# Attention with mixed heads and two dense stages on one core: where the splits of q and k, the conversion of w3 and the fold stand in the order of work

## The chip, the cores and the metric

The kernel runs on one core of one Trainium2 chip. The metric is the device time of one launch in microseconds, as the median of several runs. Beside it one execution was taken by the hardware profiler; its rows are what the argument rests on.

## What is computed

Four batches of attention (12 heads, 448 positions, 64 per head) whose scores are mixed across heads before and after the softmax, then two dense stages on the 1792 rows that come out. Shortened:

```python
scores = scale * np.matmul(q, k.transpose(0, 1, 3, 2))
scores = np.einsum('bhij,hg->bgij', scores, w_pre)
scores = scores - np.max(scores, axis=-1, keepdims=True)
attn = np.exp(scores)
attn = attn / (np.sum(attn, axis=-1, keepdims=True) + 1e-09)
attn = np.einsum('bhij,hg->bgij', attn, w_post)
x = np.matmul(attn, v)          # then laid out as 1792 x 768
a = x @ w1                      # 768 x 1024
b = x @ w2
h = a * b @ w3                  # 1024 x 1024
x2 = h @ w_out                  # 1024 x 768
h2 = x2 @ w_in                  # 768 x 2048
out = np.maximum(0.01 * h2, h2) @ w_out2
```

All weights of the dense stages arrive as float64, read as pairs of 32-bit words, and are converted to float32 on the chip.

## The kernel before

**Splits.** A matmul in full precision is made of three with rounded operands: a copy (hi) of the operand in a rounded type, written by ScalarE (`hi_act`, L76), and the rest (lo), subtracted on VectorE (`lo_dve`, L79). `split` (L82) issues both, one behind the other. The profile puts them at L77 and L80.

**Attention** (L118). Its instructions keep the order in which they are written (`manual_schedule`); each engine works through its own in that order. A batch has four chunks of query rows, three of 120 and one of 88 rows; a chunk has blocks of 10 rows, 12 blocks or 9, 180 in all. Blocks are written (b, c, t): batch, chunk, block of the chunk. For a block, `premix` (L227) mixes scores across heads by a matmul into `pm`, takes the maximum `mx` on VectorE and the exponential `e` with its sum on ScalarE; `sums` and `weigh` (L245, L249) turn the sum into weights `kr` by way of GpSimd (POOL); three blocks later (LAG) `postmix` (L260) mixes back into `po` and copies it to `ap`, on ScalarE for odd steps that are plain, otherwise on VectorE. `pm` and `po` have two PSUM banks each.

Scores come from `qk` (L184), two chunks ahead: a step computes two pairs of heads into `pq`, four copies to a tile `s` follow, and SP stores `s` to `sdr` in HBM; there are three tiles `s`. `relayout` (L211) loads them back as `sr`, for two blocks at a time, eight blocks ahead. Scores are computed at t in QT = (0, 6, 9), or (0, 5, 7) in the chunk with 9 blocks. The product with v, `av` (L279, tile `px`), of the chunk before comes in two halves at t = 3 and 4 (AT).

Around these stand the steps that feed them: `q_load` at t = 0 and `q_split` at t = 8 for the chunk three ahead; `k_load` of the next batch at t = 1, 2, 3 of chunk 1, `k_split` at its t = 7 to 11 and at t = 1 of chunk 2; `v_prep` (v's load) at t = 5 of chunk 0, and for the first batch ahead of the first scores of chunk 1. `conversions` (L303) turns w_out and w3 into float32 in HBM (`wof`, `w3f`) in 32 units of one copy `wc` on ScalarE (L96) and four operations on VectorE (L98 to L107): two steps of it at every t in QT or AT from block 14 on.

**Dense stages** (L416). Here a scheduler orders the instructions on each engine by its own estimate. `fold` (L436) multiplies w3 with w_out into `w34`, so that h is multiplied once: it loads the eight parts of `wof` (copies on ScalarE, subtractions on POOL, L442), and takes w3 in eight pieces, 48 matmuls `pw` each. In the same time `make_x` (L522) loads and splits the attention's result as x. Raw weights, `wof` and pieces of `w3f` share three buffers (tag `wr`). The scheduler was free to put the fold's loads and copies between the attention's last blocks.

Of the kernel before, what the change touches and what calls it, by code (L numbers as in the profile page):

```python
# [23 lines left out]
def attention_moe_kernel(ctx: ExitStack, tc, qt, kt, vt, w_pre, w_post, w1, w2, w3t, w_out, w_in2, w_out2, out):  # L24
# [39 lines left out]
    w3f = dram.tile([DF, DF], F32, name="w3f")  # L64
# [52 lines left out]

    def attention():  # L118
        with ExitStack() as es:
# [56 lines left out]
            def q_split(b, c):  # L176
                m = cols[c]
                qs = kv.tile([P, NPAIR, 2, CH], F32R, tag="qs", name="qs", bufs=2)
                t = qls.pop((b, c))
                hi_act(qs[:, :, 0, :m], t[:, :, :m])  # L180
                lo_dve(qs[:, :, 1, :m], t[:, :, :m], qs[:, :, 0, :m])
                qst[b, c] = qs

            def qk(b, c, p):  # L184
# [3 lines left out]
                if r == 0:  # L188
                    st[b, c] = big.tile([CH, 2 * HP, S], F32, tag="s", name="s", bufs=3)
# [21 lines left out]
            def relayout(n):  # L211
# [4 lines left out]
                if t % 2 == 0:  # L216
# [4 lines left out]
                    else:  # L221
                        nc.sync.dma_start(out=pair[:nb * H, 0], in_=sdr[b, c][o:o + nb].rearrange("i h j -> (i h) j"))
# [26 lines left out]
            def weigh(n):  # L249
# [5 lines left out]
                nc.gpsimd.tensor_scalar(  # L255
# [88 lines left out]
            filler = conversions()  # L344

# [6 lines left out]
            q_split(0, 0)  # L352
            k_split(0, 0)
            for p in range(NPAIR):
                if p + 1 < NPAIR:
                    k_split(0, p + 1)
                qk(0, 0, p)
                flush()
            q_split(0, 1)
            constants()  # L360
            for n in range(AHEAD):
                relayout(n)
            v_prep(0)
# [3 lines left out]
            q_split(0, 2)  # L367
            for n in range(NB + LAG):
                flush()
                plain = True  # L370
                if n < NB:
                    b, c, t, _ = blocks[n]
                    ci = order.index((b, c))
                    QT = (0, 6, 9) if len(chunks[c][2]) > 9 else (0, 5, 7)
# [12 lines left out]
                if m >= 0:  # L387
# [3 lines left out]
                    postmix(m, nc.scalar.copy if plain and n % 2 else nc.vector.tensor_copy)  # L391
                if n < NB:
                    if t == 0 and ci + QAHEAD + 1 < len(order):
                        q_load(*order[ci + QAHEAD + 1])
                    if t == 8 and ci + QAHEAD + 1 < len(order):
                        q_split(*order[ci + QAHEAD + 1])
                    if c == 0 and t == 5 and b > 0:
                        v_prep(b)
                    if b + 1 < B:
                        if c == NC - 3 and 1 <= t < 4:  # L400
                            k_load(b + 1, t - 1)
                        if c == NC - 3 and t >= 7:
                            k_split(b + 1, t - 7)
                        if c == NC - 2 and t == 1:
                            k_split(b + 1, 5)
                    if n >= START and not plain:
                        for _ in range(2):
# [8 lines left out]
    def moe():  # L416
        with ExitStack() as es:
# [117 lines left out]
            fold(unit)  # L535
# [108 lines left out]
```

## Time and profile before

| | us |
|---|---|
| median of 3 runs (lowest, highest) | 1443.58 (1442.26, 1443.80) |
| the profiled execution's own time | 1446.14 |
| its span, first to last instruction | 1444.2 |
| TensorE matmuls busy | 1371.5 (95%) |
| VectorE busy | 873.4 (60%) |
| ScalarE busy | 604.4 (42%) |
| GpSimd busy | 167.9 (12%) |

TensorE is the busy engine, and it is so over the whole span only on average: from about 550 us on it has no pause, ahead of that it has some in nearly every stretch. The granted clock of TensorE has a mean of 0.982 of full speed over the span, so there are stretches at half speed. The DMA engines are busiest in the attention. Engines off TensorE's path are idle much of the time; what counts of them is whether TensorE waits for what they make.

### The profile page before, as it was taken

How to read it: one execution, taken by the hardware profiler on the slowest of the kernel's cores; microseconds unless marked ns; L12 is line 12 of the kernel's file. 1: busy time of each engine (PE TensorE's matmuls, PEld its weight loads, DVE VectorE, ACT ScalarE, POOL GpSimd, SP SyncE). 2: the span in 40 equal slices, each digit the busy share in tenths (PEclk: the TensorE clock that was granted, in tenths of full speed). 3: DMA queues.
4: the chain of work that ended last, by engine and by line, in shares of the span. 5: the costliest groups of instructions: out<-in, count | busy, mean ns of one | idle time of the engine just before them, and what ended most of it. 6: DMA issues, size and time to landing. Idle time of an engine off the chain costs nothing.

```text
span 1444.2 us, 22126 instructions
## 1 busy us (share of the span) xinstructions
PE 1371.5 (95%) x8520; PEld 1184.1 (82%) x8520; DVE 873.4 (60%) x1530; ACT 604.4 (42%) x1167; POOL 167.9 (12%) x374
## 2 busy tenths in 40 slices
PE   5879997998999899999999999999999999999998
PEld 3646675766666579999999999999999999999998
DVE  4445665666666453466434967869566247686862
ACT  3545454664555443333322543525233224452330
POOL 0313232332323550000000000000000000000000
PEclk9899999999999899999999999999999999999999
DMA  8877996899798736633222434325442133432401
GB/s 238 260 202 189 278 286 192 239 294 271 199 297 260 200 103 189 200 100 107 59 86 97 129 112 132 91 95 169 151 129 88 44 109 104 137 113 85 153 1 77
DMA packets 140117, 226.23 MB, mean 157 GB/s; under 512 B 19245, under 2 KB 117549, under 8 KB 139565
## 3 DMA queue, kind: packets, MB, share of 16 engines
q1 hardware_dynamic: 140012, 224.83, 51.4%
q8 instruction: 67, 1.10, 0.3%
q14 instruction: 38, 0.30, 0.1%
HBM read 164.77 MB, written 60.03 MB: 156 GB/s over the span
## 4 chain that ended last, share of the span: by engine, by line
PE 80%; ACT 6%; DMA 5%; DVE 5%; issue 2%; SPq 1%; POOL 0%; ACTq 0%; DVEq 0%; POOLq 0%
PE pm L512 41%; PE po L579 16%; PE po L270 6%; PE px L290 5%; PE pw L450 5%; PE pm L233 4%; PE pq L194 3%; ACT e L240 2%; DMA sdr<-s 2%; DVE mx L237 2%; ACT s L201 1%; DMA sr<-sdr 1%; DMA wof<-wof 1%; DMA wr<-in_moe_w_out_dram 1%; ACT ap L277 1%
## 5 line engine op out<-in xcount | busy, mean ns | idle before, releaser
L512 PE MATMUL pm<-x,ws 128*128 128x448 f32 x2304 | 477.7, 368 | 0.0
L512 PEld LDWEIGHTS pm<-x,ws 128*128 128x128 f32 x2304 | 432.4, 188 | 43.3
L579 PE MATMUL po<-ws,g 128*128 128x384 f32 x1344 | 234.3, 334 | 0.0
L579 PEld LDWEIGHTS po<-ws,g 128*128 128x128 f32 x1344 | 233.2, 188 | 0.3
L270 PEld LDWEIGHTS po<-kr,e 120*112 120x112 f32 (+1 forms) x1440 | 172.6, 181 | 65.5 <-issue 50.8
L233 PE MATMUL pm<-sr,kpre 120*120 120x448 f32 x360 | 173.3, 564 | 44.3 <-ACT e L240 40.8
L240 ACT ACTIVATE e<-pm,mx 120x448 f32<-120x448 f32 x180 | 114.4, 636 | 216.2 <-DVE rc L253 197.6
L270 PE MATMUL po<-kr,e 120*112 120x120 f32 (+1 forms) x1440 | 187.8, 275 | 2.0 <-POOL kr L255 1.5
L255 POOL TENSOR_SCALAR kr<-kpost,rc 120x120 f32<-120x120 f32 x180 | 109.9, 610 | 299.4 <-DVE rc L253 261.9
L96 ACT ACTIVATE wc<-wr 128x768 f32<-128x768 f32 (+2 forms) x128 | 106.6, 836 | 85.8 <-DVE ws L80 57.9
L80 DVE TENSOR_TENSOR ws<-wc,ws 128x768 fp32r<-128x768 f32 x96 | 91.4, 954 | 82.6 <-ACT ws L77 81.4
L77 ACT ACTIVATE ws<-wc 128x768 fp32r<-128x768 f32 x96 | 80.7, 843 | 119.1 <-PE po L579 74.0
L237 DVE TENSOR_REDUCE mx<-pm 120x1 f32<-120x448 f32 x180 | 111.1, 618 | 25.2 <-PE pm L233 23.4
L277 DVE COPY ap<-po 112x480 f32<-112x480 f32 (+1 forms) x130 | 84.2, 648 | 61.1 <-PE po L270 60.1
L512 PE MATMUL pm<-h,ws 128*128 128x448 f32 x576 | 119.4, 368 | 0.0
L512 PEld LDWEIGHTS pm<-h,ws 128*128 128x128 f32 x576 | 108.1, 188 | 10.9
L107 DVE SCALAR_TENSOR_TENSOR wc<-wr,wc 128x768 uint32<-128x768 uint32 (+2 forms) x128 | 111.5, 871 | 2.0
L104 DVE SCALAR_TENSOR_TENSOR wc<-wr,wc 128x768 uint32<-128x768 uint32 (+2 forms) x128 | 110.9, 868 | 1.4
L290 PEld LDWEIGHTS px<-ap,vs 112*64 112x64 f32 x1536 | 78.0, 142 | 30.4 <-issue 15.2
L98 DVE TENSOR_SCALAR wc<-wc 128x768 f32<-128x768 f32 (+2 forms) x128 | 65.6, 513 | 53.7 <-ACT wc L96 53.7
L233 PEld LDWEIGHTS pm<-sr,kpre 120*120 120x120 f32 x360 | 53.2, 188 | 51.9 <-ACT e L240 47.0
L194 PEld LDWEIGHTS pq<-ks,qs 64*120 64x120 f32 (+1 forms) x576 | 51.3, 189 | 52.2 <-issue 24.3
(46 smaller groups left out, 1080.4 us busy)
## 6 DMA issues: line engine op xcount, KB each, us to landing
sr<-sdr SPq DMA_DIRECT2D x88, 420.0 KB, 8.1
sdr<-s SPq DMA_DIRECT2D x36, 840.0 KB, 6.6
wr<-in_moe_w_dram SPq DMA_DIRECT2D x32, 768.0 KB, 4.6
wr<-in_moe_w_in_dram SPq DMA_DIRECT2D x32, 768.0 KB, 4.6
wr<-in_moe_w_out_dram SPq DMA_DIRECT2D x32, 768.0 KB
wr<-in_moe_w_dram SPq DMA_DIRECT2D x16, 512.0 KB, 8.2
sdr<-s SPq DMA_DIRECT2D x12, 616.0 KB
wr<-in_moe_w_out_dram SPq DMA_DIRECT2D x16, 384.0 KB, 7.5
```

The source lines that it names most:

```text
L96: nc.scalar.activation(out=cf, in_=hi.bitcast(F32), func=ACTF.Abs)
L104: lambda: nc.vector.scalar_tensor_tensor(out=c, in0=hi, scalar=0xC0000000, in1=c, op0=ALU.bitwise_and, op1=ALU.bitwise_or),
L107: lambda: nc.vector.scalar_tensor_tensor(out=c, in0=lo, scalar=29, in1=c, op0=ALU.logical_shift_right, op1=ALU.bitwise_or),
L233: nc.tensor.matmul(pm[:r], kpre[:r, :nb, :].rearrange("p i h -> p (i h)"), sr[:r], start=True, stop=True)
L237: nc.vector.tensor_reduce(out=mx[:r], in_=pm[:r], axis=AX.X, op=ALU.max, negate=True)
L240: nc.scalar.activation(out=e[:r], in_=pm[:r], func=ACTF.Exp, bias=mx[:r], scale=1.0, accum_out=sm[:r])
L255: nc.gpsimd.tensor_scalar(out=kr[:r], in0=kpost[:r], scalar1=rc[:r], scalar2=None, op0=ALU.mult)
L270: nc.tensor.matmul(po[:, jc, :, :nb], e[:r, jc * JP:(jc + 1) * JP], kr[:r, :, :nb], start=True, stop=True,)
L277: copy(ap[:, :, :, o:o + nb], po[:, :, :, :nb])
L290: nc.tensor.matmul(px[e * D:(e + 1) * D, p - p0, :ni], vst[b][:, jc, 2 * p + e, :], ap[:, jc, 2 * p + e, :ni], start=(jc == 0), stop=(jc = ...
L512: nc.tensor.matmul(dst, wt[:, a, kk, :], x[:, kk, c, n * S:(n + 1) * S], start=(kk == 0 and j == 0), stop=(kk == kn - 1 and j == 2),)
L579: nc.tensor.matmul(po, g[:, m, a, t * P:(t + 1) * P], wts[m][:, c, 0, cs], start=(m == 0 and j == 0), stop=(m == FQ - 1 and j == 2),)
```

## The change

- `k_split` and `q_split` issue only the copy on ScalarE and return the subtraction, which the loop issues behind the step's postmix (`lows`). q's split stands at t = 3 (t = 8 in the first chunk), k's at t = 4 of chunk 1 (two) and t = 3 and 4 of chunk 2 (two each).
- `q_load` stands at t = 8, one chunk earlier; `k_load` at t = 0, 1, 6; `v_prep` at t = 4 of chunk 0, in the first batch too; only four relayouts stand ahead of the scores of chunk 1. In the first chunk QT is (5, 8, 10). `s` has four tiles.
- `conversions` has only the 16 units of w_out. A step in AT issues one step of it, one in QT two.
- ScalarE copies `ap` at t = 1, 5, 8, 10 where the step is plain.
- The fold loads w3 raw, 1 MB a piece, and converts it like the other weights. Its instructions on POOL and SP stand behind the attention's last `kr` and its last relayout of a single block.

```diff
 def k_split(b, p):
     kst[b, p] = kv.tile([P, 2, S], F32R, tag="ks", name="ks", bufs=NPAIR + 2)
-    split(kst[b, p], kls[b, p // 2][:, p % 2, :])
+    src, dst = kls[b, p // 2][:, p % 2, :], kst[b, p]
+    hi_act(dst[:, 0], src)
+    return lambda: lo_dve(dst[:, 1], src, dst[:, 0])
...
-    st[b, c] = big.tile([CH, 2 * HP, S], F32, tag="s", name="s", bufs=3)
+    st[b, c] = big.tile([CH, 2 * HP, S], F32, tag="s", name="s", bufs=4)
...
 units = [(w_out, wof, r, c0, DM // 2) for r in range(DF // P) for c0 in (0, DM // 2)]
-units += [(w3t, w3f, r, c0, DF // 2) for r in range(DF // P) for c0 in (0, DF // 2)]
...
-for n in range(AHEAD):
+for n in range(4):
     relayout(n)
-v_prep(0)
 for p in range(NPAIR):
     qk(0, 1, p)
     flush()
+for n in range(4, AHEAD):
+    relayout(n)
...
+if t == (LAG if ci else 8) and ci + QAHEAD + 1 < len(order):
+    lows.append(q_split(*order[ci + QAHEAD + 1]))
+if b + 1 < B and t in AT:
+    if c == NC - 3 and t == LAG + 1:
+        lows += [k_split(b + 1, p) for p in (0, 1)]
+    if c == NC - 2:
+        lows += [k_split(b + 1, p) for p in ((2, 3) if t == LAG else (4, 5))]
...
-postmix(m, nc.scalar.copy if plain and n % 2 else nc.vector.tensor_copy)
+postmix(m, nc.scalar.copy if plain and n < NB and t in (1, 5, 8, 10) else nc.vector.tensor_copy)
+while lows:
+    lows.pop(0)()
...
-w = {"w1": w1, "w2": w2, "wi": w_in2}[kind]
-return load_raw(wp, col_block(w, m), (KM, P), 3)
+w = {"w1": w1, "w2": w2, "wi": w_in2, "w3t": w3t}[kind]
+return load_raw(wp, col_block(w, m), (KF if kind == "w3t" else KM, P), 3)
...
-fold(unit)
+with tc.issue_after(ends["pool"].ins), tc.issue_after(ends["sync"].ins):
+    fold(unit)
```

First place, ScalarE in chunk (1, 1). Before, from t = 8 on (a number behind a name is that of the tile):

```order
L240 ACTIVATE e_2342,sm_2343<-pm_2338,mx_2340 120x448
L277 COPY ap_2188<-po_2352 112x48x10
L77 ACTIVATE qs_2358<-ql_2099 128x6x120
L77 ACTIVATE ks_2361<-kl_2125 128x448
L240 ACTIVATE e_2368,sm_2369<-pm_2364,mx_2366 120x448
L201 ACTIVATE s_2376<-pq_2377 88x448
L201 ACTIVATE s_2376<-pq_2378 88x448
L201 ACTIVATE s_2376<-pq_2387 88x448
L201 ACTIVATE s_2376<-pq_2388 88x448
L77 ACTIVATE ks_2403<-kl_2147 128x448
L240 ACTIVATE e_2416,sm_2417<-pm_2412,mx_2414 120x448
```

After, the same engine at t = 3 and 4 of chunk (1, 2):

```order
L243 ACTIVATE e_2514,sm_2515<-pm_2510,mx_2512 120x448
L76 ACTIVATE qs_2522<-ql_2341 128x6x120
L76 ACTIVATE ks_2524<-kl_2108 128x448
L76 ACTIVATE ks_2526<-kl_2108 128x448
L95 ACTIVATE wc_2566<-wr_2299 128x384
L243 ACTIVATE e_2572,sm_2573<-pm_2568,mx_2570 120x448
L76 ACTIVATE ks_2582<-kl_2295 128x448
L76 ACTIVATE ks_2584<-kl_2295 128x448
L243 ACTIVATE e_2626,sm_2627<-pm_2622,mx_2624 120x448
```

The copies of k, which stood one to a step between an exponential and the next, now stand two together, with q's, in the steps with the product with v.

Second place, SP after the first chunk's scores are stored. Before:

```order
L220 DMA sr_229<-sdr_0_0_57 120x2x448
L220 DMA sr_231<-sdr_0_0_57 120x2x448
L220 DMA sr_233<-sdr_0_0_57 120x2x448
L220 DMA sr_235<-sdr_0_0_57 120x2x448
L170 DMA vs_237<-in_v_dram 112x3072
L209 DMA sdr_0_1_58<-s_239 120x1792
L209 DMA sdr_0_1_58<-s_261 120x1792
L209 DMA sdr_0_1_58<-s_283 120x1792
L220 DMA sr_316<-sdr_0_0_57 120x2x448
```

After:

```order
L223 DMA sr_228<-sdr_0_0_57 120x2x448
L223 DMA sr_230<-sdr_0_0_57 120x2x448
L212 DMA sdr_0_1_58<-s_232 120x1792
L212 DMA sdr_0_1_58<-s_254 120x1792
L212 DMA sdr_0_1_58<-s_276 120x1792
L223 DMA sr_298<-sdr_0_0_57 120x2x448
L223 DMA sr_300<-sdr_0_0_57 120x2x448
L223 DMA sr_313<-sdr_0_0_57 120x2x448
L177 DMA ql_315<-in_q_dram 128x720
L223 DMA sr_341<-sdr_0_0_57 120x2x448
L223 DMA sr_374<-sdr_0_1_58 120x2x448
L173 DMA vs_382<-in_v_dram 112x3072
```

Two relayouts and v's load, which stood ahead of the stores of chunk 1, now stand behind them.

Third place, ScalarE at the seam between attention and fold. Before:

```order
L240 ACTIVATE e_5833,sm_5834<-pm_5829,mx_5831 120x448
L277 COPY ap_5759<-po_5841 112x48x10
L240 ACTIVATE e_5851,sm_5852<-pm_5847,mx_5849 120x448
L240 ACTIVATE e_5869,sm_5870<-pm_5865,mx_5867 96x448
L277 COPY ap_5759<-po_5877 112x48x10
L77 ACTIVATE ws_6028<-wf_6022 128x1024
L77 ACTIVATE ws_6033<-wf_6024 128x1024
L77 ACTIVATE ws_6094<-wf_6026 128x1024
L277 COPY ap_5759<-po_5893 112x48x10
L77 ACTIVATE x_6127<-xm_6128 128x448
L77 ACTIVATE x_6127<-xm_6160 128x448
```

After:

```order
L76 ACTIVATE wo_5844<-wof_5865 128x768
L76 ACTIVATE wo_5844<-wof_5869 128x768
L76 ACTIVATE x_6000<-xm_6001 128x448
L76 ACTIVATE x_6000<-xm_6033 128x448
L76 ACTIVATE wo_5844<-wof_5873 128x768
L95 ACTIVATE wc_5883<-wr_5877 128x1024
L95 ACTIVATE wc_5894<-wr_5879 128x1024
L76 ACTIVATE x_6000<-xm_6076 128x448
L76 ACTIVATE x_6000<-xm_6108 128x448
L76 ACTIVATE ws_5889<-wc_5883 128x1024
```

Before, eight copies of `wof` stand further up, among the exponentials, and the first copies of w3's pieces (`ws`) follow the last exponential. After, three stand further up and five behind the last exponential (three of them here), then two conversions of w3's pieces (`wc`) and copies of x, and then the first copy `ws`. On POOL the eight subtractions of `wof` stood among the last blocks and now stand in a row behind the last `kr`.

## Rows read from the trace of the kernel before

**Rows 1.** Chain of waits, merged: start us, us, what (with number of pieces).

```profile
44.98 1.49 PE pm L233 x2
...
52.94 0.82 PE po L270 x8
...
54.52 0.82 PE po L270 x8
...
59.27 0.82 PE po L270 x8
...
148.05 1.00 PE po L270 x8
...
152.42 1.00 PE po L270 x8
...
172.49 2.04 PE px L290 x48
...
201.57 2.68 PE px L290 x48
...
239.95 3.92 PE px L290 x48
...
299.83 2.04 PE px L290 x48
...
456.19 2.68 PE px L290 x48
...
522.88 2.68 PE px L290 x48
...
549.96 62.27 PE pw L450 x358
```

**Rows 2.** Timeline of PE, 62 to 116 us: first product of chunk (0,1).

```profile
68.80 2.68 PE L290 MATMUL px<-ap,vs 112*64 112x120 f32 x48
```

**Rows 3.** Waits of PE, 0 to 550 us: total us, times, longest.

```profile
PE pm L233 <- ACT e L240: 40.8, 26, 10.7
```

**Rows 4.** Windows: busy us of each engine, then PEclk, DMA share, GB/s.

```profile
40.00:45.00 5.00, 3.47 (x11) 2.61 (x12) 0.86 (x3) 2.81 (x8) 1.67 (x5) 0.50 0.95 332
...
400.00:450.00 50.00, 47.08 (x430) 34.09 (x427) 33.79 (x75) 26.65 (x66) 15.60 (x36) 1.00 0.97 293
```

**Rows 5.** The tile kl: k copies, k subtractions, their waits, landing of k loads.

```profile
L77 ACT ACTIVATE ks<-kl x24: 560/576/622, 5.3 to 364.9; 128x448 fp32r<-128x448 f32 x24
...
L80 DVE TENSOR_TENSOR ks<-kl,ks x24: 617/624/626, 5.9 to 365.5; 128x448 fp32r<-128x448 f32 x24
...
  ACT ks L77: 25.0, 18
...
DMA to landing us min/median/max: 4.1/8.4/12.7
```

**Rows 6.** Groups by shape, 0 to 560 us: count | busy us, mean ns | idle before.

```profile
L442 POOL TENSOR_TENSOR wo<-wof,wo 128x768 fp32r<-128x768 f32 x8 | 14.4, 1805 | 8.4 <-DMA wof<-wof 6.7 <-ACT wo L77 1.5
...
L96 ACT ACTIVATE wc<-wr 128x512 f32<-128x512 f32 x16 | 11.1, 691 | 0.0
...
L104 DVE SCALAR_TENSOR_TENSOR wc<-wr,wc 128x512 uint32<-128x512 uint32 x16 | 10.9, 681 | 0.0
```

**Rows 7.** Timelines of SP and ACT: start us, us, [idle before <- releaser].

```profile
23.55 1.28 SPq L209 DMA_DIRECT2D sdr<-s  x3
...
39.02 1.85 ACT L201 ACTIVATE s<-pq 120x448 f32<-120x448 f32 x4 [11.39 <-DMA sdr<-s]
...
81.66 0.54 ACT L96 ACTIVATE wc<-wr 128x384 f32<-128x384 f32 x1 [11.46 <-DMA wr<-in_moe_w_out_dram]
```

**Rows 8.** Timeline of POOL: two kr, beside VectorE's L104 and last.

```profile
480.57 1.59 POOL L255 TENSOR_SCALAR kr<-kpost,rc 120x120 f32<-120x120 f32 x1 [0.40 <-PE po L270]
...
538.56 0.58 POOL L255 TENSOR_SCALAR kr<-kpost,rc 96x120 f32<-96x120 f32 x1 [0.36 <-DVE rc L253]
```

**Rows 9.** Page, DMA issues: count, KB each, median us to landing.

```profile
wr<-in_moe_w_dram SPq DMA_DIRECT2D x32, 768.0 KB, 4.6
```

More of the change, by code (lines that the diff above doesn't have):

```diff
@@ L116, in convert @@
         return cf
+    ends = {}
     def attention():
@@ L179, in q_split @@
                 t = qls.pop((b, c))
+                qst[b, c] = qs
                 hi_act(qs[:, :, 0, :m], t[:, :, :m])
-                lo_dve(qs[:, :, 1, :m], t[:, :, :m], qs[:, :, 0, :m])
-                qst[b, c] = qs
+                return lambda: lo_dve(qs[:, :, 1, :m], t[:, :, :m], qs[:, :, 0, :m])
             def qk(b, c, p):
@@ L221, in relayout @@
                     else:
-                        nc.sync.dma_start(out=pair[:nb * H, 0], in_=sdr[b, c][o:o + nb].rearrange("i h j -> (i h) j"))
+                        ends["sync"] = nc.sync.dma_start(out=pair[:nb * H, 0], in_=sdr[b, c][o:o + nb].rearrange("i h j -> (i h) j"))
                     srt[n] = pair[:, 0, :]
@@ L254, in weigh @@
                 kr = wk.tile([IB * H, H, IB], F32, tag="kr", name="kr", bufs=4)
-                nc.gpsimd.tensor_scalar(
+                ends["pool"] = nc.gpsimd.tensor_scalar(
                     out=kr[:r], in0=kpost[:r], scalar1=rc[:r], scalar2=None, op0=ALU.mult
@@ L344, in attention @@
             filler = conversions()
+            lows = []
             q_load(0, 0)
@@ L351, in attention @@
             q_load(0, 2)
-            q_split(0, 0)
-            k_split(0, 0)
+            q_split(0, 0)()
+            k_split(0, 0)()
             for p in range(NPAIR):
                 if p + 1 < NPAIR:
-                    k_split(0, p + 1)
+                    k_split(0, p + 1)()
                 qk(0, 0, p)
                 flush()
-            q_split(0, 1)
+            q_split(0, 1)()
             constants()
-            for n in range(AHEAD):
+            for n in range(4):
                 relayout(n)
-            v_prep(0)
             for p in range(NPAIR):
@@ L366, in attention @@
                 flush()
-            q_split(0, 2)
+            for n in range(4, AHEAD):
+                relayout(n)
+            q_split(0, 2)()
             for n in range(NB + LAG):
@@ L373, in attention @@
                     ci = order.index((b, c))
-                    QT = (0, 6, 9) if len(chunks[c][2]) > 9 else (0, 5, 7)
+                    QT = (5, 8, 10) if ci == 0 else (0, 6, 9) if len(chunks[c][2]) > 9 else (0, 5, 7)
                     plain = t not in QT and t not in AT
@@ L390, in attention @@
                         av(*blocks[m - tt - 1][:2], tt)
-                    postmix(m, nc.scalar.copy if plain and n % 2 else nc.vector.tensor_copy)
+                    postmix(m, nc.scalar.copy if plain and n < NB and t in (1, 5, 8, 10) else nc.vector.tensor_copy)
+                while lows:
+                    lows.pop(0)()
                 if n < NB:
[L393 to L397, printed above, removed]
-                        v_prep(b)
[L399 to L405, printed above, removed]
+                    if c == 0 and t == 4:
+                        v_prep(b)
+                    if (t == 8 or n == 0) and ci + QAHEAD + (1 if n == 0 else 2) < len(order):
+                        q_load(*order[ci + QAHEAD + (1 if n == 0 else 2)])
+                    if b + 1 < B and c == NC - 3 and t in (0, 1, 6):
+                        k_load(b + 1, (0, 1, 6).index(t))
                     if n >= START and not plain:
-                        for _ in range(2):
+                        next(filler, None)
+                        if t in QT:
                             next(filler, None)
@@ L463, in load_w @@
             def load_w(kind, m):
-                if kind in ("w34", "w3t"):
+                if kind == "w34":
                     t = wp.tile([P, KF, P], F32, tag="wr", name="wf", bufs=3)
-                    src = w3f if kind == "w3t" else w34
-                    nc.sync.dma_start(out=t, in_=src[:, m * P:(m + 1) * P].rearrange("(k p) m -> p k m", p=P))
+                    nc.sync.dma_start(out=t, in_=w34[:, m * P:(m + 1) * P].rearrange("(k p) m -> p k m", p=P))
                     return t
```

5 lines of the change are left out of this document (2 added, 3 removed).

## Prediction

> **What bounds the kernel now.** I read the chain of waits first. From 549.96 us on it is TensorE alone: the rest of the fold's 384 matmuls (358 in 62.27 us) and then the dense stages without a break [rows 1]. The change adds no matmul there, so all it can win lies in the attention ahead of it, and all it can lose there too or at the seam.
>
> In the attention I price a chunk as if TensorE never waited. A plain step is 54.52 - 52.94 = 1.58 us. Two steps of which one computes scores take 59.27 - 54.52 = 4.75, so scores add 1.59. A step with the product with v takes 152.42 - 148.05 = 4.37, so it adds 2.79 [rows 1]. A chunk of 12 blocks with three groups of scores and two products is 12 x 1.58 + 3 x 1.59 + 2 x 2.79 = 29.3 us, one of 9 blocks 24.6, one of 12 without scores 24.5. The reader should now look at the first product with v of each chunk, which stands at t = 3 and so marks the chunks. 172.49 to 201.57 is 29.1: as priced. 201.57 to 239.95, the chunk that carries five of the six k splits, is 38.4. Summed over marks [rows 1, 2]: 68.80 to 172.49 takes 103.7 against 83.2 (20.5 lost), 172.49 to 299.83 takes 127.3 against 112.5 (14.8), 299.83 to 456.19 takes 156.4 against 141.8 (14.6), 456.19 to 522.88 takes 66.7 against 53.8 (12.9). That is **62.8 us** above the price of TensorE's own work. TensorE's waits for the exponentials e are 40.8 us of it in 26 waits [rows 3]; the rest is smaller waits and the clock, which is granted at 0.50 (1.2 GHz) after a long wait [rows 4]. Attention is therefore bound by TensorE in quiet chunks and by the in-order queues of ScalarE and VectorE in busy ones.
>
> **The change, part by part.** *Splits.* Now a k split puts its subtraction on VectorE right behind its copy on ScalarE: VectorE waited 25.0 us in 18 places for these copies, and in its queue the next block's maximum stands behind the subtraction, and e behind that [rows 5]. The step becomes a loop through two engines. Afterwards q's and k's copies stand in the two steps with the product with v, and the subtractions behind that step's copies out of PSUM. Does it fit? The fullest such step has one q and two k splits. ScalarE: two k copies at 0.576, a q copy (720 columns for 448, so 0.93) and one conversion of at most 0.69 [rows 5, 6], 2.8 us. VectorE: two at 0.624, q 1.0, one conversion step of at most 0.68, 2.9 us. The product with v gives 2.79 us of TensorE's time [rows 1]: just covered, and a chunk has only two such steps. If the cover is gone, each microsecond over it is a microsecond of TensorE. The bounds are nothing left of the loss and all of it; I take 0.25 us left in each of 12 chunks (3 us), since the chunk at 172.49, which has conversions and a q split and no k split, already runs as priced. The q split is also earlier: the first scores of a batch no longer wait for a split issued one step before.
>
> *Start.* ScalarE waits 11.39 us until 39.02 for a store out of the score tiles, because four relayouts and v's load were queued on SP ahead of the stores issued at 23.55, and three buffers were taken [rows 7]. With four buffers, two relayouts and no v ahead of the stores, and chunk 2's scores moved from t = 0 to t = 5, blocks 0 to 3 no longer wait for it. Block 4 now waits instead: its relayout (0.43 MB, 120 x 896 floats) is queued behind two others and three stores of 0.86 MB (120 x 1792). 3.9 MB from about 22 us at 250 to 293 GB/s (the latter what a full window moves [rows 4]) land at 35 to 38 us. Block 4's premix then starts near 37.5 where it stood at 44.98 [rows 1], 7.5 earlier, but has one group of scores more behind it (1.59): a gain of 6 (3 to 9).
>
> *Conversions.* Half of the units (w3: 8.4 MB read, 4.2 MB written) leave the attention, and one unit's step is issued in the steps with v where there were two. ScalarE's 11.46 us wait at 81.66 for the first raw weight [rows 7] shrinks, since the load now has a whole step with v before it is used, but doesn't vanish: I leave 4 us (0 to 8) of that chunk's loss. What moves into the fold is costed there.
>
> *k loads.* They move from t = 1, 2, 3 to t = 0, 1, 6, and the first two splits from t = 7, 8 to t = 4. Landing took 4.1 to 12.7 us, median 8.4 [rows 5]; from the end of t = 0 to t = 4 there are about 2 x 1.58 + 4.37 + 1 = 8.5. A late one stops ScalarE by up to 4 us, three times; TensorE is two blocks ahead. Costed at nothing, 12 at most.
>
> *The fold queues behind the attention.* Before, its loads and copies stand among the last blocks, and ScalarE waits there for wof: the 12.9 us above. After, three loads are issued behind the last relayout, and two copies still stand eight exponentials before the end. With scores and their stores done a load of this size should land in little more than the 4.1 us that a k load took at least [rows 5]. TensorE can go on for two blocks (3.2 us), so 4 us (1 to 8) of the 12.9 stay.
>
> Now the price. The eight subtractions on POOL, 1.805 us each [rows 6], all start behind the last kr. Let T be its end, 538.56 + 0.58 = 539.1 before [rows 8]. Before, TensorE's fold block starts in effect at 549.96 less 26 matmuls of 62.27/358 = 0.174, 545.4, or T + 6.3. After: three buffers serve wof and the raw w3, so the first piece of w3 is loaded when the sixth subtraction is done (six of 1.805, and half a microsecond of waiting, T + 11.3) and the second at T + 13.6. A piece is 1 MB; 768 KB take 4.6 us [rows 9]. Both pieces, 2.1 MB, are there at T + 19 (293 GB/s) to T + 24 (768 KB in 4.6 us); I take T + 21. On ScalarE the copy of piece one stands behind the conversion of piece two and two copies of x (the third place in the change's section): 1.4 + 1.2 + 1.4 us at most, by twice the 512-column row and the 448-column row. TensorE starts at T + 25 (T + 21 to T + 31). That is 18.7 us later against T than before. It then runs at the low clock for a while: the window from 40 to 45, in which a long wait ends, is wholly at 0.50 [rows 4]; 3 us. **21.7 us lost** (17 to 30).
>
> Later pieces are covered: 48 matmuls take 8.35 us, a piece costs VectorE five operations of at most 1.36 us (twice 0.681 [rows 6]), 6.8 us.
>
> A rule weighed: POOL's kr takes 1.59 us beside VectorE's L104 and 0.58 alone [rows 6, 8]. The Trainium skill, "SBUF — State Buffer", section "Who interferes with whom", says that a GpSimd operation and a VectorE operation with two SBUF inputs exclude each other for a whole instruction; the trace agrees, with these 1.59 us. By it the two subtractions for x that VectorE does beside POOL's eight would delay the fold by up to 2 x 0.62 = 1.2 us, and the sum would be 1408 instead of 1407.
>
> **Sum.** Attention: 62.8 - 3 - 4 - 4 + 6 = 57.8 us won. Seam: 21.7 lost. Net 36.1. The profiled execution took 1446.1 (span 1444.2 and 1.9 around it), 2.5 above the median of 1443.6; the same work is gone from either, so I take it off the median: **1407**, 1410 for a profiled execution.
>
> **Rivals.** *The stalls move (0.17).* The steps with v are filled to 2.9 of 2.79 us, and k loads may land late. If half of the three losses of 14.6 to 20.5 stays (about 17 us with the late loads), 1407 + 17 = 1424. For it: the cover is that thin. Against: the next steps are plain and have slack on both engines.
>
> *A better seam and start (0.14).* If SP's queue is idle at the end, the w3 pieces land at T + 17 and the fold starts at T + 20, and the two waits that I left (4 and 4) go too: 1407 - 13 = 1394.
>
> *The fold is fed too slowly (0.05), slower than before.* ScalarE and SP work in order, and in the fold a piece's copy stands among copies of x and of results. Traffic is 8.4 MB of w3, 2.8 of x and 3.1 of results in 67 us, 213 GB/s, against 167 GB/s for one load alone (768 KB in 4.6 us). If pieces come every 13 us instead of 8.35, and TensorE idles at each, eight cost 37 us, the whole gain: the point from which it decides. At 13.5 the time is 1407 + 41 = 1448.
>
> *The attention is set by DMA (0.04).* A full window has a DMA share of 0.97 [rows 4]. If transfers set the chunks, the moved splits win nothing before the conversions end, and only the 12.6 MB taken out count, 12.6/0.293 = 43 us less: the start's 6 and the tail's 9 would be in it, so 1444 - 43 + 22 = 1423. Against: the chunks that run as priced have the same share.
>
> **How the numbers follow.** Forecast, 1397 to 1418: 0.60. The seam's bounds (17 to 30) and the start's (3 to 9) make most of its width. Rivals 0.17, 0.14, 0.05, 0.04. The range 1388 to 1428 takes in all but the slow fold and the tails of the others, about 0.15. About 0.2% (3 us) is what a measurement of this kernel can tell from no change. Faster 0.94, within it 0.01, slower 0.05.
>
> **What would show it.** Right: marks 29 to 30 us apart in chunks with 12 blocks, no wait over 2 us on e between 100 and 460, SP's stores of chunk 1 ahead of v, one gap of 15 to 25 us on TensorE before the fold's first matmul, then 66 to 70 us of fold and dense stages as long as before. Wrong: waits on e in the steps after t = 3 and 4, ScalarE waiting for kl, gaps on TensorE inside the fold.

## The result

| | before | after |
|---|---|---|
| median (lowest, highest), us | 1443.69 (1442.26, 1446.25) | 1403.22 (1398.96, 1403.41) |
| ratio, 95% interval | | 0.9711 [0.9688, 0.9734] |
| profiled execution, us | 1446.14 | 1403.05 |
| its span, us | 1444.2 | 1401.3 |

The change is faster by 40.5 us in the medians and by 42.9 in the spans of the profiled executions. The prediction was 1407, with 1388 to 1428 around it.

### The profile after

In the changed kernel the maximum `mx` is L240, `e` L243, `kr` L258, the products with v L293, the splits L76 (copy) and L79 (subtraction), the conversion L95 to L106, `wof`'s subtractions on POOL L449 and the fold's matmuls L457. The page gives TensorE as busy for 97% of the span where it was 95%. Its row of granted clocks (40 slices of 35 us, in tenths of full speed) is below 9 in the first slice, the start, and in the two around 490 us, the seam, and nowhere between.

```profile
PEclk8999999999999879999999999999999999999999
```

The chain of waits (start, us, what) gives the marks of the prediction, the first product with v of a chunk, to be set beside [rows 1]:

```profile
37.23 1.82 PE pm L236 x2
...
64.18 2.68 PE px L293 x48
...
148.42 2.01 PE px L293 x48
...
261.51 2.01 PE px L293 x48
...
401.51 2.68 PE px L293 x48
...
429.27 2.68 PE px L293 x48
...
456.22 2.68 PE px L293 x48
...
500.80 68.54 PE pw L457 x380
```

64.18 to 148.42 takes 84.2 us against a price of 83.2, then 113.1 against 112.5, 140.0 against 141.8, and 54.7 against 53.8. From the first mark to the last the chunks run 0.7 us above the price of TensorE's own work, where they ran 62.8 above it. That 0.7 is a net figure: the price is not exact for each chunk. The one at 401.51 took 27.8 us against a price of 29.3, and the one at 429.27 took 27.0 against 24.5. From the fold's end on (500.80 + 68.54 = 569.34) 832.0 us are left to the end of the span, as many as before (1444.2 less 612.23 [rows 1]): the dense stages did not change, and the whole difference lies ahead of them.

TensorE's waits (what it waited for; us in total, times, longest) to 560 us, which answer to [rows 3]:

```profile
PE pm L236 <- DMA sr<-sdr: 8.5, 2, 5.7
...
PE pm L236 <- ACT e L243: 2.8, 3, 2.0
```

The 40.8 us of waits for exponentials are 2.8. Waits for relayouts are 8.5 us; the longer of the two, 5.7, is the one on block 4 that the prediction expected at the start. One new wait of 20.3 us stands in front of the fold. The views of POOL, SP, ScalarE, VectorE and TensorE show how it is built:

```profile
471.89 0.58 POOL L258 TENSOR_SCALAR kr<-kpost,rc 96x120 f32<-96x120 f32 x1 [0.36 <-DVE rc L256]
472.45 5.37 POOL L449 TENSOR_TENSOR wo<-wof,wo 128x768 fp32r<-128x768 f32 x3
478.17 3.56 POOL L449 TENSOR_TENSOR wo<-wof,wo 128x768 fp32r<-128x768 f32 x2 [0.36 <-ACT wo L76]
482.10 1.80 POOL L449 TENSOR_TENSOR wo<-wof,wo 128x768 fp32r<-128x768 f32 x1 [0.37 <-ACT wo L76]
...
483.93 3.20 SPq L87 DMA_DIRECT2D wr<-in_moe_w_dram  x2
...
492.23 1.12 ACT L95 ACTIVATE wc<-wr 128x1024 f32<-128x1024 f32 x1 [4.89 <-DMA wr<-in_moe_w_dram]
...
485.34 1.86 DVE L79 TENSOR_TENSOR x<-xm,x 128x448 fp32r<-128x448 f32 x1 [6.71 <-ACT x L76]
493.39 0.69 DVE L97 TENSOR_SCALAR wc<-wc 128x1024 f32<-128x1024 f32 x1 [5.65 <-ACT wc L95]
...
474.29 3.86 PE L293 MATMUL px<-ap,vs 112*64 112x88 f32 x96 [0.65 <-DVE ap L280]
498.47 1.65 PE L457 MATMUL pw<-wo,ws 128*128 128x384 f32 x4 [20.32 <-ACT ws L76]
500.80 11.51 PE L457 MATMUL pw<-wo,ws 128*128 128x384 f32 x51 [0.68 <-DVE ws L79]
```

Read it from the last `kr`, which ends at 472.47 (T). POOL does six of its subtractions; with the sixth a buffer comes free at 483.90, and SP asks for w3's first piece at 483.93. ScalarE has it at 492.23, VectorE converts from 493.39, TensorE, which ended the attention's last product (474.29) at 478.15, starts at 498.47, T + 26.0. Windows of the fold (busy us of PE, PEld, DVE, ACT and POOL, granted clock, DMA share, GB/s) show it starting at half the clock (1.2 GHz), which it has back by 506:

```profile
498.50:505.00 6.50, 5.83 (x17) 5.32 (x18) 5.80 (x7) 1.31 (x2) 0.00 (x0) 0.50 0.71 236
506.00:540.00 34.00, 34.00 (x197) 34.00 (x197) 31.50 (x37) 19.22 (x27) 0.00 (x0) 1.00 0.82 264
```

### The profile page after: what moved, and what is told of

Same layout as the page of the kernel before. It is cut to its first block, busy times and chain, and to the rows that moved or that the text cites. A ratio compares the mean times of both kernels' runs of the same rounds, so it can differ in the third digit from the quotient of the medians.

```text
span 1401.3 us, 22086 instructions
## 1 busy us (share of the span) xinstructions
PE 1355.2 (97%) x8520; PEld 1176.5 (84%) x8520; DVE 873.7 (62%) x1496; ACT 606.6 (43%) x1161; POOL 162.8 (12%) x374
## 4 chain that ended last, share of the span: by engine, by line
PE 95%; DMA 2%; DVE 1%; ACT 1%; POOL 1%; issue 0%; SPq 0%; POOLq 0%; DVEq 0%
PE pm L518 42%; PE po L586 17%; PE po L273 11%; PE pm L236 9%; PE px L293 5%; PE pq L197 5%; PE pw L457 5%; DMA sr<-sdr 1%; DMA wof<-wof 1%; DMA wr<-in_moe_w_dram 1%; POOL wo L449 1%; DMA kl<-in_k_dram 0%; DVE wc L103 0%; ACT wo L76 0%; ACT s L204 0%
## 5 line engine op out<-in xcount | busy, mean ns | idle before, releaser
L273 PEld LDWEIGHTS po<-kr,e 120*112 120x112 f32 (+1 forms) x1440 | 168.8, 177 | 60.2 <-issue 54.9
L243 ACT ACTIVATE e<-pm,mx 120x448 f32<-120x448 f32 x180 | 114.1, 634 | 192.7 <-DVE rc L256 183.1
L273 PE MATMUL po<-kr,e 120*112 120x120 f32 (+1 forms) x1440 | 183.9, 271 | 0.4 <-ACT ap L280 0.4
L236 PE MATMUL pm<-sr,kpre 120*120 120x448 f32 x360 | 169.1, 553 | 11.4 <-DMA sr<-sdr 8.5
L79 DVE TENSOR_TENSOR ws<-wc,ws 128x768 fp32r<-128x768 f32 (+1 forms) x104 | 101.3, 976 | 88.0 <-ACT ws L76 86.8
L240 DVE TENSOR_REDUCE mx<-pm 120x1 f32<-120x448 f32 x180 | 111.9, 622 | 45.7 <-PE pm L236 39.8
L76 ACT ACTIVATE ws<-wc 128x768 fp32r<-128x768 f32 (+1 forms) x104 | 89.2, 859 | 118.2 <-PE po L586 73.9
L95 ACT ACTIVATE wc<-wr 128x768 f32<-128x768 f32 (+2 forms) x120 | 104.8, 876 | 81.8 <-DVE ws L79 67.3
L258 POOL TENSOR_SCALAR kr<-kpost,rc 120x120 f32<-120x120 f32 x180 | 105.7, 587 | 277.7 <-DVE rc L256 187.8
L106 DVE SCALAR_TENSOR_TENSOR wc<-wr,wc 128x768 uint32<-128x768 uint32 (+2 forms) x120 | 110.1, 918 | 1.4
L293 PEld LDWEIGHTS px<-ap,vs 112*64 112x64 f32 x1536 | 74.6, 137 | 22.7 <-issue 10.5
L457 PE MATMUL pw<-wo,ws 128*128 128x384 f32 x384 | 70.2, 345 | 21.0 <-ACT ws L76 20.3
```

What stands on the lines that cost most here:

```text
L106: lambda: nc.vector.scalar_tensor_tensor(out=c, in0=lo, scalar=29, in1=c, op0=ALU.logical_shift_right, op1=ALU.bitwise_or),
L236: nc.tensor.matmul(pm[:r], kpre[:r, :nb, :].rearrange("p i h -> p (i h)"), sr[:r], start=True, stop=True)
L240: nc.vector.tensor_reduce(out=mx[:r], in_=pm[:r], axis=AX.X, op=ALU.max, negate=True)
L243: nc.scalar.activation(out=e[:r], in_=pm[:r], func=ACTF.Exp, bias=mx[:r], scale=1.0, accum_out=sm[:r])
L258: ends["pool"] = nc.gpsimd.tensor_scalar(out=kr[:r], in0=kpost[:r], scalar1=rc[:r], scalar2=None, op0=ALU.mult)
L273: nc.tensor.matmul(po[:, jc, :, :nb], e[:r, jc * JP:(jc + 1) * JP], kr[:r, :, :nb], start=True, stop=True,)
```

## The experiments

Ten kernels, each the changed kernel with one part put back or moved (e8 adds an edit to e7's, e10 makes four at once). Ratios are to the kernel before on the same chip; 0.001 is 1.4 us. The changed kernel has 0.9711.

### The place of the splits and their division

**e1_splits_back**: the splits of q and k at their old steps and in one piece, behind the postmix.

```diff
-if t == (LAG if ci else 8) and ci + QAHEAD + 1 < len(order):
-    lows.append(q_split(*order[ci + QAHEAD + 1]))
-if b + 1 < B and t in AT:
...
+if t == 8 and ci + QAHEAD + 1 < len(order):
+    q_split(*order[ci + QAHEAD + 1])()
+if b + 1 < B and c == NC - 3 and t >= 7:
+    k_split(b + 1, t - 7)()
+if b + 1 < B and c == NC - 2 and t == 1:
+    k_split(b + 1, 5)()
```

> The changed kernel with q's and k's splits back in their old steps (q at t = 8, k at t = 7 to 11 of chunk 1 and t = 1 of chunk 2), copy and subtraction together behind the postmix; all else as changed. Theory (a split in a plain step of 1.58 us makes a loop through ScalarE and VectorE that TensorE waits for): the chunk with five k splits takes 37 to 39 us between marks again instead of 30, and the first scores of a batch wait again, in all 28 to 38 us more, 1431 to 1441. Rival (those waits came from w3's conversions and their transfers in the same queues, which are gone here too): at most 6 more, under 1410.

Measured: 1438.65, ratio 0.9967 [0.9947, 0.9987]. With the splits back, nearly the whole gain is gone, about 37 us, as its theory expected. The chunk of batch 1 that carries five k splits takes 37.8 us between marks (188.11 to 225.95), where the changed kernel has 30.5 (176.75 to 207.22). The timeline (start, us, [idle before <- what released it]) shows the loop that the prediction spoke of, in chunk (1,1):

```profile
209.32 0.63 ACT L243 ACTIVATE e<-pm,mx 120x448 f32<-120x448 f32 x1 [1.64 <-DVE rc L256]
...
209.95 1.82 ACT L204 ACTIVATE s<-pq 88x448 f32<-88x448 f32 x4
...
211.64 0.59 ACT L76 ACTIVATE ks<-kl 128x448 fp32r<-128x448 f32 x1
...
212.26 0.62 DVE L79 TENSOR_TENSOR ks<-kl,ks 128x448 fp32r<-128x448 f32 x1 [2.41 <-ACT ks L76]
212.81 0.55 DVE L103 SCALAR_TENSOR_TENSOR wc<-wr,wc 128x384 uint32<-128x384 uint32 x1
213.39 0.56 DVE L106 SCALAR_TENSOR_TENSOR wc<-wr,wc 128x384 uint32<-128x384 uint32 x1
213.87 0.62 DVE L240 TENSOR_REDUCE mx<-pm 120x1 f32<-120x448 f32 x1
...
214.58 0.63 ACT L243 ACTIVATE e<-pm,mx 120x448 f32<-120x448 f32 x1 [1.91 <-DVE rc L256]
...
215.36 1.01 PE L236 MATMUL pm<-sr,kpre 120*120 120x448 f32 x2 [3.42 <-ACT e L243]
```

From one `e` to the next the work goes ScalarE (four copies of scores, `ks`), VectorE (`ks`, two conversion steps, the maximum), ScalarE: 5.26 us. TensorE, two blocks ahead, waits 3.42 us for it.

**e2_old_place_two_parts**: the old steps, but in two parts: the copy ahead of the step's scores and postmix, the subtraction behind the postmix.

```diff
...
+if t == 8 and ci + QAHEAD + 1 < len(order):
+    lows.append(q_split(*order[ci + QAHEAD + 1]))
+if b + 1 < B and c == NC - 3 and t >= 7:
+    lows.append(k_split(b + 1, t - 7))
+if b + 1 < B and c == NC - 2 and t == 1:
+    lows.append(k_split(b + 1, 5))
```

> As the kernel before this one, but in two parts: the copy ahead of the step's postmix, the subtraction behind it; still in the old plain steps. If it is the loop through two engines that costs, dividing it is nearly enough: 3 to 10 us over the changed kernel, since VectorE then has 0.62 + 0.16 + 0.65 + 0.62 = 2.05 us in a step of 1.58. If it is the place (no TensorE work that covers the split), it stays as slow as undivided: 28 to 38 over.

Measured: 1422.86, ratio 0.9852 [0.9833, 0.9871], between the two expectations: at the old place the division, with the earlier copy that comes with it, wins back about 16 of the 37 us. The same steps of this kernel say why:

```profile
205.46 0.63 ACT L243 ACTIVATE e<-pm,mx 120x448 f32<-120x448 f32 x1 [1.18 <-DVE rc L256]
206.08 0.56 ACT L76 ACTIVATE ks<-kl 128x448 fp32r<-128x448 f32 x1
...
206.54 1.81 ACT L204 ACTIVATE s<-pq 88x448 f32<-88x448 f32 x4
...
208.99 0.63 ACT L243 ACTIVATE e<-pm,mx 120x448 f32<-120x448 f32 x1 [0.20 <-DVE rc L256]
209.61 0.56 ACT L76 ACTIVATE ks<-kl 128x448 fp32r<-128x448 f32 x1
...
210.21 0.62 DVE L79 TENSOR_TENSOR ks<-kl,ks 128x448 fp32r<-128x448 f32 x1 [1.25 <-ACT ks L76]
...
210.75 0.62 DVE L240 TENSOR_REDUCE mx<-pm 120x1 f32<-120x448 f32 x1
...
211.47 0.63 ACT L243 ACTIVATE e<-pm,mx 120x448 f32<-120x448 f32 x1 [0.83 <-DVE rc L256]
```

The copy `ks` now stands ahead of the copies of scores, so their 1.8 us are out of the loop: 3.53 us instead of 5.26. But e, `ks`, `ks`, `mx` remain in a row, and without conversions or scores that is 211.47 - 208.99 = 2.48 us for a step in which TensorE has 1.58 us of work. What the division can't do is give the loop a step that is long enough.

**e3_new_place_one_piece**: the new steps, but copy and subtraction both behind the postmix.

```diff
-lows.append(q_split(*order[ci + QAHEAD + 1]))
+q_split(*order[ci + QAHEAD + 1])()
...
-lows += [k_split(b + 1, p) for p in ((2, 3) if t == LAG else (4, 5))]
+for p in ((2, 3) if t == LAG else (4, 5)):
+    k_split(b + 1, p)()
```

> The changed kernel with the splits in the new steps (those with the product with v), but each split in one piece behind the postmix. If the place is what counts, 0 to 2 us over the changed kernel (1403 to 1405). If the division is what counts, 15 or more over.

Measured: 1400.65, ratio 0.9702 [0.9686, 0.9719]: not told apart from the changed kernel, and not slower. In the steps with the product with v the division is worth nothing; the place alone wins all that place and division win together.

**e9_four_in_one_step**: the four k splits of chunk 2 at t = 3, with q's.

```diff
-lows += [k_split(b + 1, p) for p in ((2, 3) if t == LAG else (4, 5))]
+lows += [k_split(b + 1, p) for p in ((2, 3, 4, 5) if t == LAG else ())]
```

> The changed kernel with the four k splits of chunk 2 all at t = 3, beside q's, where it has two at t = 3 and two at t = 4. Theory of the prediction (a step with the product with v covers about 2.79 us of copies, and what is over it is lost on TensorE): the step holds four k copies at 0.58, a q copy at 0.93 and one conversion of at most 0.69 on ScalarE (3.9 us), 4.2 us on VectorE, so each of three batches loses 1.1 to 1.4 us, 4 us in all: 1406 to 1409. Rival (cover is the slack of the several steps that stand around the copies, not that of one step, since TensorE is two blocks ahead and the next step has a product with v too): nothing is lost, 1401 to 1405.

Measured: 1403.51, ratio 0.9711 [0.9680, 0.9743]. Nothing is lost, although the step holds, by the sum in its expectation, 3.9 us on ScalarE and 4.2 on VectorE beside 2.79 us of the product. The chunk concerned takes 29.7 us in batch 1 in either kernel (206.85 to 236.56 here, 207.22 to 236.92 in the changed one). The trace shows VectorE at work without a pause from 210.58 to 217.9 us and ScalarE waiting 4.05 us in front of the next exponential, and in the same time no wait in TensorE's rows: it has the second product, at 211.22, to do. The rival holds: what covers is not that step alone. The prediction's test of fit, one step's copies against one product, was too strict. The two products of a chunk are 5.6 us together; no run tried more than that.

### The start

**e4_start_back**: three tiles `s`, all relayouts and v's load ahead of chunk 1's stores, the old QT in the first chunk.

```diff
-st[b, c] = big.tile([CH, 2 * HP, S], F32, tag="s", name="s", bufs=4)
+st[b, c] = big.tile([CH, 2 * HP, S], F32, tag="s", name="s", bufs=3)
...
-for n in range(4):
+for n in range(AHEAD):
     relayout(n)
+v_prep(0)
...
-QT = (5, 8, 10) if ci == 0 else (0, 6, 9) if len(chunks[c][2]) > 9 else (0, 5, 7)
+QT = (0, 6, 9) if len(chunks[c][2]) > 9 else (0, 5, 7)
...
```

> The changed kernel with the start as before: eight relayouts and v's load ahead of the scores of chunk 1, three score tiles, scores of chunk 2 at t = 0, 6, 9. My prediction priced the start at 6 us (3 to 9): 1406 to 1412, with a wait of about 11 us on ScalarE until 39 us. Rival (the moved start only trades one wait for a wait on block 4's relayout): within 2 us of the changed kernel.

Measured: 1407.75, ratio 0.9749 [0.9733, 0.9766], about 5 us over the changed kernel. On TensorE the wait is back:

```profile
41.50 1.85 PE L236 MATMUL pm<-sr,kpre 120*120 120x448 f32 x2 [10.45 <-ACT e L243]
```

In the changed kernel TensorE waits 5.71 us for a relayout instead, in front of the row at 37.23.

### The seam

**e5_w3_early**: w3 converted in the attention again, at two steps of conversion in each step that computes scores or a product; the fold still behind the attention.

```diff
 units = [(w_out, wof, r, c0, DM // 2) for r in range(DF // P) for c0 in (0, DM // 2)]
+units += [(w3t, w3f, r, c0, DF // 2) for r in range(DF // P) for c0 in (0, DF // 2)]
...
-next(filler, None)
-if t in QT:
+for _ in range(2):
     next(filler, None)
...
```

> The changed kernel, but w3 is converted to HBM within the attention again (two steps of conversion at every step that computes scores or the product with v, 32 units), and the fold reads half as much; the fold still queues behind the attention. Theory (the copies of k and q were the stall, conversions were not; what the new seam costs is the POOL chain, the load and the conversion of w3's first piece): the attention keeps marks 28 to 30 us apart and its loss grows by 10 us at most, the gap before the fold falls from 20.3 us to 12 to 15: 1396 to 1409. Rival (the 16 units taken out of the attention are where its gain came from): chunks of 32 us and more come back in the batches that now convert, and the time is 1415 or more.

Measured: 1405.33, ratio 0.9721 [0.9697, 0.9745], not told apart. TensorE's rows at the seam:

```profile
484.83 3.86 PE L294 MATMUL px<-ap,vs 112*64 112x88 f32 x96 [0.65 <-DVE ap L281]
501.65 3.57 PE L458 MATMUL pw<-wo,ws 128*128 128x384 f32 x10 [12.96 <-ACT ws L77]
```

The wait is 12.96 instead of 20.32, 7.4 less, but the last product with v starts at 484.83; in the changed kernel it starts at 474.29, 10.5 earlier. So the conversions of w3 cost the attention about what they spare the fold. No chunk takes over 30.6 us: the 10 us are spread over many. Where the conversions stand is nearly without effect on the whole, and the rival's 1415 is ruled out.

**e6_fold_free**: without the rule that holds the fold behind the attention.

```diff
-with tc.issue_after(ends["pool"].ins), tc.issue_after(ends["sync"].ins):
-    fold(unit)
+fold(unit)
```

> The changed kernel without the rule that puts the fold's work on POOL and SP behind the attention's last kr and last relayout. All eight copies of wof then stand among the last thirty exponentials, and ScalarE is done with them before w3's pieces come. Theory (the rule wins about 9 us in the tail and loses most of 18.7 at the seam, because the buffers of w3 wait for POOL): the tail loses 5 to 10 us again, with TensorE waiting for e behind copies that wait for wof, and the gap before the fold falls to 5 to 10 us: 1395 to 1406. Rival (the rule itself is worth the gain of the last chunk): the tail loses over 13 us and the gap stays over 12, since w3 must be loaded raw and converted anyway: 1408 to 1420.

Measured: 1397.09, ratio 0.9664 [0.9649, 0.9678], 6 to 7 us **faster** than with the rule.

```profile
427.86 2.68 PE L293 MATMUL px<-ap,vs 112*64 112x120 f32 x48
...
481.07 3.86 PE L293 MATMUL px<-ap,vs 112*64 112x88 f32 x96 [0.65 <-DVE ap L280]
491.35 1.65 PE L457 MATMUL pw<-wo,ws 128*128 128x384 f32 x4 [6.42 <-ACT ws L76]
```

The tail loses as expected, with a wait on e of 3.54 us in front of the premix at 447.11: from the product at 427.86 to the last one are 53.2 us, in the changed kernel 45.0 (429.27 to 474.29). At the seam 6.4 us of wait stand where 20.3 stood. The rule wins 8 us and costs more: of the parts of the change that were put back, it is the one without which the kernel is faster.

**e7_wof_own**: `wof` lands in the buffers of another group, so that w3's first loads wait for no subtraction.

```diff
-t = wp.tile([P, DM], F32, tag="wr", name="wof", bufs=3)
+t = so.tile([P, DM], F32, tag="ws", name="wof")
```

> The changed kernel, but the eight parts of wof land in the four buffers of another group than w3's raw pieces, so that w3's first three loads wait for no subtraction on POOL; they then stand ahead of wof on SP, right behind the last relayout. Theory (the first piece of w3 was late because its buffer came free with POOL's sixth subtraction): w3 is there when the last exponential is done, TensorE starts at about 12 us after the last kr and is paced by POOL's subtractions (8 x 1.8 us) until about 18 us after it, in effect 14 us behind the last kr where it is 26: 1391 (1387 to 1396). Rival (DMA or ScalarE's queue sets the start, not the buffers): wof then lands later by what w3 landed earlier, the start moves by 4 us at most: 1399 to 1404.

Measured: 1391.41, ratio 0.9624 [0.9610, 0.9639], about 12 us faster than the changed kernel. SP asks for three pieces of w3 at 448.89, 35 us earlier. The size came out as expected, the reason behind it not:

```profile
463.17 14.07 SPq L447 DMA_DIRECT2D wof<-wof  x2
...
472.95 3.86 PE L293 MATMUL px<-ap,vs 112*64 112x88 f32 x96 [0.65 <-DVE ap L280]
484.75 1.65 PE L457 MATMUL pw<-wo,ws 128*128 128x384 f32 x4 [7.93 <-ACT ws L76]
490.43 14.80 PE L457 MATMUL pw<-wo,ws 128*128 128x384 f32 x72 [4.03 <-DVE ws L79]
...
482.01 2.83 DVE L103 SCALAR_TENSOR_TENSOR wc<-wr,wc 128x1024 uint32<-128x1024 uint32 x1
...
481.20 8.09 POOL L449 TENSOR_TENSOR wo<-wof,wo 128x768 fp32r<-128x768 f32 x3 [6.16 <-ACT wo L76]
```

TensorE starts at 484.75, T + 13.6 (T is 471.14 here), but POOL did not pace it from T + 12 on. The second load of `wof` stood on SP until the last product with v was done (14.07 us for two issues), POOL had one subtraction at 473.22 and the next at 481.20, and from there on both engines slowed each other: VectorE's operation took 2.83 us where the one at 480.87 took 1.22, POOL's 8.09/3 = 2.70 where the one at 473.22 took 1.82. The second wait, 4.03 us, is for VectorE's subtraction `ws` behind these. Not all of the gain lies at the seam: from the product at 430.24 to the last one (472.95) are 42.7 us, 2.3 less than in the changed kernel, since ScalarE has no `wof` to wait for in between.

**e8_wof_own_dve**: as e7, with the subtractions on VectorE.

```diff
-nc.gpsimd.tensor_tensor(out=wo[:, kk, 1], in0=t, in1=wo[:, kk, 0].bitcast(F32), op=ALU.subtract)
+lo_dve(wo[:, kk, 1], t, wo[:, kk, 0])
```

> As the kernel with buffers of their own for wof, and the eight subtractions for wof on VectorE instead of POOL. Theory (POOL's pace of 1.8 us sets the start once the loads are free): VectorE takes about 1 us for each, but has the conversions of two pieces (about 10 us with their subtractions) in the same queue, so the start is 0 to 4 us earlier than with POOL: 1387 to 1395. Rival (VectorE becomes the bound, since everything of the seam now goes through it): the start is later than with POOL's help by 3 us or more: 1395 to 1400.

Measured: 1390.23, ratio 0.9619 [0.9605, 0.9633], not told apart from e7. VectorE's operations are 1.22 again, but the eight subtractions, 0.95 each, now stand among them. The first wait is 9.5 us (7.9 in e7), the second 1.6 (4.0 in e7), so neither engine's pace alone sets the start. What the start waits for shows in the next kernel's rows.

**e10_in_place_early**: `wof` lands where its rest will stand, w3's pieces are asked for first, the rule on SP takes an earlier relayout, and VectorE subtracts.

```diff
+if t == 2:
+    ends["sync"] = load
...
+fill()
 for kk in range(KF):
-    t = wp.tile([P, DM], F32, tag="wr", name="wof", bufs=3)
+    t = wo[:, kk, 1].bitcast(F32)
...
-nc.gpsimd.tensor_tensor(out=wo[:, kk, 1], in0=t, in1=wo[:, kk, 0].bitcast(F32), op=ALU.subtract)
+lo_dve(wo[:, kk, 1], t, wo[:, kk, 0])
```

> The changed kernel, but the parts of wof land in the place of their own rest (no buffer is shared with w3), three pieces of w3 are asked for ahead of them, the rule on SP holds the fold behind an earlier relayout (that of blocks 2 and 3 of the last chunk), and the subtractions stand on VectorE, with most of wof's copies and subtractions in the two steps with the product with v of the last chunk. Theory (the fold waits for a chain of loads and of copies that could run under the last blocks): the tail loses 1 to 4 us, and the gap before the fold falls to 7 to 9 us (y's copies, then the conversion of w3's first piece, 5.2 us on VectorE, and its copy): 1383 to 1390. Rival (what wins at the seam is lost in the tail, where VectorE is busy for 1.43 of 1.58 us in a plain step): the tail loses 6 us or more: 1391 to 1398.

Measured: 1391.43, ratio 0.9628 [0.9595, 0.9662], just above the theory's range and at the lower end of the rival's.

```profile
478.17 3.86 PE L295 MATMUL px<-ap,vs 112*64 112x88 f32 x96 [0.65 <-DVE ap L282]
488.46 1.65 PE L460 MATMUL pw<-wo,ws 128*128 128x384 f32 x4 [6.43 <-ACT ws L76]
...
482.08 0.43 DVE L302 COPY y<-px 128x264 f32<-128x264 f32 x1 [1.39 <-PE px L295]
482.43 0.69 DVE L97 TENSOR_SCALAR wc<-wc 128x1024 f32<-128x1024 f32 x1
...
486.09 1.22 DVE L106 SCALAR_TENSOR_TENSOR wc<-wr,wc 128x1024 uint32<-128x1024 uint32 x1
...
487.35 1.06 ACT L76 ACTIVATE ws<-wc 128x1024 fp32r<-128x1024 f32 x1 [1.41 <-DVE wc L106]
```

The wait at the seam is 6.4 us, the shortest with the rule in force, and the last product starts 5.2 us later than in e7 (478.17 against 472.95). What is won at the seam is paid in the tail: from the product at 429.78 to the last one are 48.4 us, 3.4 more than in the changed kernel (the theory said 1 to 4) and 5.7 more than in e7. The rows also show what is left of the wait. ScalarE's part of the conversion was done at 477.6, but on VectorE the conversion stands behind the copies `y` of the last product. Six operations follow from 482.43 to 487.31, two of them for the second piece, then the copy `ws`, then TensorE. The same six stand behind `y` in e7 (477.21 to 482.09) and in e6, where the wait is 6.42; in e8 two of the subtractions stand among them. A conversion ahead of `y` was not tried. The three kernels of 1390 to 1391 beat both the kernel before and the changed one, by three ways of cutting the same wait.

## Why the prediction was right

The forecast was the right case, by the right mechanism, and 4 us too high. Two errors of opposite sign lie behind the sum: the attention won 8.8 us more than forecast, the seam lost 2.1 more. That they cancel in part is luck. Its steps:

- **Attention.** Predicted 57.8 us won, measured 66.6: T came at 472.47 instead of 539.1. It is the 62.8 of loss less 0.7 that is left, and 4.6 at the start.
- **What is left, the term that was mis-sized: 11 predicted, 0.7 measured.** Of the 4 left for `wof` in the tail 2.0 came as a wait on e, the longest of three (the chunk it stands in, from 429.27, is 2.4 above its price). Of the 4 left for the first conversion's load ScalarE waited 2.4 us, and the whole stretch from 64.18 lost 1.0 of TensorE's time. The 3 left in twelve chunks (0.25 each) are not to be seen. This last rested on a step that is "just covered" at 2.9 of 2.79 us; e9 put 4.2 us there at no cost. VectorE's wait for the copies `ks` fell from 25.0 us [rows 5] to 1.3.
- **Start.** Predicted 6, measured 68.80 - 64.18 = 4.6; e4 gives about 5. Block 4's premix stands at 37.23, predicted 37.5. From there to the first mark are 27.0 us instead of 23.8; one more group of scores explains 1.6 of these 3.1. The rest is the clock, by this estimate: it is granted at 0.50 from 37 to 41 us and 0.79 from 41 to 43, so at half speed for about 4.6 us behind that premix; before, at 0.59 from 45 to 47 and at 1.00 from 47 on, for about 1.7. Half of the difference is 1.5 us. The prediction priced the half clock at the seam and left it out here.
- **k loads.** Costed at nothing, and they cost nothing: ScalarE's only wait for `kl`, 0.8 us, is for the first batch's, within the first 8 us of the span, and none is for a load that was moved.
- **Seam.** Predicted 21.7 us lost, measured 23.8: the start is at T + 26.0 (T + 25 predicted, T + 6.3 before), 19.7; the fold's 384 matmuls take 569.34 - 498.47 = 70.9 against 66.8 at 0.174 each, 4.1, of which 0.7 is a wait; the 3.4 that remain fit the low clock (3 predicted), at which 17 matmuls took 5.83 us, 0.34 each. The chain came link by link: sixth subtraction, buffer, load, conversion, copy. It was also tried: with other buffers (e7) the time falls by about 12 us.
- **Sum.** 66.6 - 23.8 = 42.8, the 42.9 of the spans; predicted 36.1, so the profiled execution is 7 us under the forecast's 1410. The medians differ by 40.5, because the profiled execution before lay 2.5 us above its median; there the forecast is 4 us off.
- **The rule weighed.** The Trainium skill, "SBUF — State Buffer", section "Who interferes with whom", says that a VectorE operation with two SBUF inputs and a GpSimd operation that reads SBUF exclude each other. The trace agrees: the first of the two subtractions for x, begun at 485.34 while POOL's seventh ran (484.92 to 486.72), took 1.86 us, the second 0.61; in e8, where POOL has nothing to do there, such a one takes 0.62. But VectorE then had nothing to do until 493.39, so the 1.2 us that the prediction gave as the rule's price cost nothing here. In e7, where both engines had work in a row, it did (2.83 for 1.22).
- **The rivals.** *The stalls move* would have shown as waits on e in the steps behind t = 3 and 4; there are 2.8 us in the whole attention. *A better seam and start*: one half of it came, the losses left at 4 and 4 fell to about 2 and 1, but the seam was no better (T + 26.0, not T + 20). *Fed too slowly*: TensorE waits once in the fold, 0.68 us. *Set by DMA*: e3 and e1 move the same bytes in the same loads and lie 38 us apart, which transfers alone can't explain.

By parts, from the runs: the place and division of the splits are worth about 37 us, the start 5, w3's conversion in the fold nothing that can be told, and the rule that queues the fold behind the attention is worth -6 to -7. In the attention alone these parts don't make up the whole: T, 472.5 in the changed kernel and 539.1 before, is 508.6 in e1, 477.2 in e4, 483.0 in e5 and 479.3 in e6, later by 36, 5, 10.5 and 7 us, which is 58 of the 66.6. The other 8 or 9 stay open: no run put back by itself which steps copy `ap` on ScalarE, or the earlier loads of q, k and v, and parts put back singly need not add up.

## What to carry to other kernels

Where two in-order engines hand work back and forth once a step, look for the loop from one block's exponential to the next. Here a copy and a subtraction put into that loop made a step of 2.48 us out of one in which TensorE has 1.58 us of work, though neither of the two is the busy engine. In the steps in which TensorE had other work they cost nothing, divided or not, and with two or with four k splits in one step; more was not tried. When work is queued behind a stage to keep it out of that stage's way, list what now starts at the stage's end in sequence, and above all which buffers are shared along that sequence: here a shared group of three buffers made the load of the first operand wait for six subtractions, and one line that took other buffers won 12 us. When the load is early, look at the next engine's queue: here the conversion stood on VectorE behind a copy that needs the stage's last product.

## What the runs showed that was not expected

In e7 POOL and VectorE slow each other to nearly the sum of their times, 3.04 us: beside POOL's subtractions (1.82 us alone) VectorE's operation with two SBUF inputs took 2.83 instead of 1.22, and POOL's took 2.70. Moving the work to one engine (e8) brought the times back, but TensorE's first matmul of the fold came no earlier (T + 15.2, against T + 13.6).

A buffer of another group was not free either: in e7 the second load of `wof` was issued only when the last product with v was done, at 476.9. That the new buffer lies where v or `ap` still lay would fit this; no run tested it.
